# Decode attention: key, value and head-weight loads split by partitions over two DMA queues

## The chip, the cores and the metric

The kernel runs on one core of a Trainium2 chip. The metric is the time of one execution on the device, in microseconds (us); the median of three runs of the kernel before is 1301.6 us (1301.52 to 1301.69). A core has TensorE (PE in the profile), VectorE (DVE), ScalarE (ACT), GpSimd (POOL) and SyncE (SP), which run their own instruction streams, and 16 DMA engines that move data between the device memory (HBM) and the on-chip memory of 128 partitions (SBUF). SyncE and ScalarE each have a DMA queue: an instruction on the engine issues a transfer, and the 16 DMA engines carry it out.

## The reference

One step of decoding for two sequences: a layer norm, an attention over a cache of 8192 keys and values in each of 16 heads, and a gated bilinear feed-forward block behind a second layer norm.

```
B, Sq, D = 2, 1, 448;  H, Sk, Dh = 16, 8192, 256;  F = 1792;  all float32
xn = layernorm(x)
q = (xn @ wq) as [B, H, 1, Dh]
p = softmax(einsum("bhqd,bhkd->bhqk", q, k_cache) / 16)
h = x + einsum("bhqk,bhkd->bhqd", p, v_cache) as [B, 1, H * Dh] @ wo
hn = layernorm(h)
out = h + ((hn @ w_gate) * (hn @ w_up)) @ w_down
```

The two caches are 32 x 8 MiB each; with the weights 561 MB are read once and used once.

## The kernel before

The work is a loop over 32 units, one for each head and sequence (unit i is head i // 2, sequence i % 2). A unit's keys are one transfer of 8.39 MB, 64 KB in each of 128 partitions (a partition holds 64 consecutive keys of 256 numbers), and its values are another. There are two key buffers that overlap by 16 of 64 columns, so that the next keys may be written once VectorE has read the first part of the present ones, and one value buffer.

For unit n:

1. VectorE multiplies the first quarter of the keys (16 columns) by the query and sums it, then the other three quarters; the scores go to `s`. Each part is a product (`tensor_mul`, 128x4096 or 128x12288) and a sum (`tensor_reduce`). The first product waits for the keys.
2. `softmax(n - 1)`, the softmax of the unit before, lies between the first product and the first sum: a maximum on VectorE (`nm`), a small matmul, and two ScalarE instructions (`nb`, and the exponentials `p`).
3. `mix(n - 1)`: TensorE weighs the values of the unit before with `p` into `o_ps` in 32 steps; it waits for the values (event `e_v`).
4. `mixed(n - 1)`: ScalarE copies `o_ps` to `o_sb`, TensorE turns it, ScalarE scales it to `oT`. Every second unit adds its head to the output, and every fourth computes the next queries (`queries`; ScalarE writes `q`).

All loads but that of x stand on SyncE's queue, in this order: the head weights of the first two heads, the keys of unit 0 in two transfers (24 and 40 columns), then alternately the keys of unit n + 1 (which wait for VectorE's first sum of unit n) and the values of unit n (which wait for TensorE's last use of the values of unit n - 1). Four transfers of head weights (`d_w_1` to `d_w_4`, 2.75 to 3.67 MB) stand behind keys 2, 10, 18 and 26. The values of units 27 to 31 are loaded in pieces (`LATE`; `EARLY` = `LOOP` = 27 is the first of these units), and the feed-forward weights follow at the end. The class `Orders` keeps the instruction list of every engine and works out the semaphore waits; `load` adds one transfer to one engine's list, and a transfer adds 16 to its semaphore when it has landed. TensorE's part of units 0 to 26 is a hardware loop, which takes events by their count.

Of the kernel before, what the change touches and what calls it, by code (L numbers as in the profile page):

```python
# [10 lines left out]
B, D, H, SK, DH, F = 2, 448, 16, 8192, 256, 1792  # L11
EPS = 1e-5
P = 128
HALF = 64
# [46 lines left out]
    (slice(HALF, P), slice(DC - 1, DC), slice(DC, DC + 1)),  # L61
)


SCRATCH = 1024
ALIGN = (2048 - SCRATCH - 4 * 32) // 4
# [2 lines left out]
EARLY = NQ - len(LATE)  # L69
LOOP = EARLY  # L70
# [4 lines left out]
class Orders:  # L75
# [88 lines left out]
    def load(self, engine, name, out, in_, reads=(), writes=(), event=None):  # L164
# [11 lines left out]
        e = self.engines[engine]  # L176
        self._add(engine, (waits, lambda: e.dma_start(out, in_), (name, 16)))  # L177

    def take(self, event, n=1):

        at = self.taken[event] = self.taken.get(event, -1) + 1
        self._learn("PE", self.events[event][at])
        s, e = self.sem(event), self.nc.tensor
        self._add("PE", ({}, lambda: e.wait_ge(s, n), (event, -n)))  # L184
# [32 lines left out]
def decode_block(nc, x, k_cache, v_cache, w, wg, wu, wd, out):  # L217
    o = Orders(nc)
    o.sem("d_out")

    def sb(name, *shape):
        return nc.alloc_sbuf_tensor(name, list(shape), F32)[:]
# [12 lines left out]
    def act(out, in_, fn, r=(), w=(), event=None, **kw):  # L235
        put("ACT", "activation", out, in_, fn, r=r, w=w, event=event, **kw)

    def mm(out, lhsT, rhs, start, stop, r=(), w=(), mark=None, **kw):
        put("PE", "matmul", out, lhsT, rhs, start=start, stop=stop, r=r, w=w, mark=mark, **kw)
# [8 lines left out]
    w_sb = sb("w_sb", P, WALL)  # L248
    buffers = {"k": k_sb, "v": v_sb}
# [17 lines left out]
    def keys(cache, i, lo, hi):  # L267
        h, b = divmod(i, B)
        return cache[b, h].rearrange("(p j) d -> p j d", p=P)[:, lo:hi, :]

    def load_keys(name, cache, i, lo, hi, buf, at, event=None):
        o.load(
            "SP", name, buffers[buf][:, at : at + hi - lo, :], keys(cache, i, lo, hi),
            writes=[(buf, at * DH, (at + hi - lo) * DH)], event=event,
        )

    def k_base(i):
        return i % 2 * (NJ - OVER)

    def load_k(i, lo=0, hi=NJ):  # L280
        load_keys(f"d_k_{i}_{lo}", k_cache, i, lo, hi, "k", k_base(i) + lo)

    def v_parts(i):
        got, lo = [], 0
        for n, place in LATE[i - EARLY] if i >= EARLY else ((NJ, None),):
            buf, at = place or ("v", lo)
            got.append((lo, lo + n, buf, at))
            lo += n
        return got

    def load_v(i, part):
        lo, hi, buf, at = part
        load_keys(f"d_v_{i}_{lo}", v_cache, i, lo, hi, buf, at, "e_v" if i < LOOP else None)

    def load_w(name, k, lo, hi, event=None):
        o.load("SP", name, w_sb[:, lo:hi], w[k][:, lo:hi], writes=[("w", lo, hi)], event=event)

    def wq_at(hp):
        return hp % 2 * WQ
# [1 line left out]
    def wo_at(h):  # L301
        return 2 * WQ + h % 4 * WO
# [59 lines left out]
    for c in range(DC):  # L362
# [9 lines left out]
        w=["xc_x"],  # L372
# [14 lines left out]
    def q_at(h):  # L387
        return h % 2 * (1 + h // 2 % 2)

    for k in range(2):  # L390
        for b in range(B):
            for c in range(DC):
                at = c * 2 * DH + (k * DH if c < DC - 1 else 0)
# [3 lines left out]
                    w=[f"q_ps{b}"], mark="PE" if c == DC - 1 else None,  # L397
                )
            at = q_at(k)
# [19 lines left out]
    def other(i):  # L419
        return i % 2 if i >= LOOP else 0  # L420

    def event(name, i):
        return name if i < LOOP else None

    def take(name, i, n=1):
        if i < LOOP:
            o.take(name, n)
# [10 lines left out]
    def common(i):  # L438
        return piece(i, always if i == 0 else gone)

    def at_turn(i):
        return piece(i, turn_of.get(i, gone))
# [9 lines left out]
    def scores(i, part, between=None):  # L452
        h, b = divmod(i, B)
        s, name = s_t[i % 2], f"s{i % 2}"
        lo, hi = score_parts(i)[part]
        at = k_base(i) + lo
        kt = k_sb[:, at : at + hi - lo, :]
        qk, there = kt, ("k", at * DH, (at + hi - lo) * DH)
        if i == 0 and part == 0:
            qk, there = v_sb[:, : hi - lo, :], ("v", 0, (hi - lo) * DH)  # L460
        q, slot = qs[b], q_at(h)
        here = ("k", at * DH, (at + hi - lo) * DH)
        dve(
            "tensor_mul", qk, kt, q[:, slot, :][:, None, :].to_broadcast([P, hi - lo, DH]),
            r=[here, (f"q{b}", slot, slot + 1)], w=[there],
        )
        if between is not None:
            between()
        dve("tensor_reduce", s[:, lo:hi], qk, axis=AX.X, op=ALU.add, r=[there], w=[(name, lo, hi)])
# [27 lines left out]
    def mix(i, parts):  # L497
        k = other(i)
        with common(i):
            take("e_v", i, 16)  # L500
            for lo, hi, buf, at in parts:
                for t in range(lo // 2, hi // 2):
                    g, j = 32 * (t % 4), at + 2 * t - lo
                    mm(
                        o_ps[k][g : g + 2, :], p_t[k][:, 2 * t : 2 * t + 2],
                        buffers[buf][:, j : j + 2, :], t < 4, t >= NJ // 2 - 4,
                        r=[f"p{k}", (buf, j * DH, (j + 2) * DH)], w=[f"o_ps{k}"],
                        mark="PE" if t == hi // 2 - 1 else None,
                    )

    def mixed(i):
        h, b = divmod(i, B)
        k = other(i)
        act(o_sb, o_ps[k], AF.Copy, r=[f"o_ps{k}"], w=["o_sb"], event=event("e_o", i))
        with common(i):
            take("e_o", i)
            for c in range(2):
                for j in range(2):
                    mm(
                        oT_ps[:, c : c + 1], o_sb[:, (2 * j + c) * P : (2 * j + c + 1) * P],  # L520
                        sel[:, j : j + 1], j == 0, j == 1, r=["o_sb", "sel"], w=["sm1"],
                        mark="PE" if c == 1 and j == 1 else None,
                    )
        act(oT[:, :, b], oT_ps, AF.Copy, scale=rl_t[i % 2], r=["sm1", f"rl{i % 2}"],
            w=[("oT", b, b + 1)], event=event("e_oT", i))
        with common(i):
            take("e_oT", i)
        if b == B - 1 and h < H - 1:
            at = wo_at(h)
            with at_turn(i):  # L530
                if i % 8 == 1:
                    take("e_w", i, 16)
                for c in range(2):
                    mm(
                        acc_ps, oT[:, c, :], w_sb[:, at + c * D : at + (c + 1) * D], False,
                        h == H - 2 and c == 1, r=["oT", ("w", at, at + WO)], w=["acc_ps"],
                        mark="PEx" if c == 1 else None,
                    )
# [48 lines left out]
    def late_guest(name, rows, *shape):  # L587
# [6 lines left out]
    pair = sb("pair", B, B, 16)  # L594
    dve("tensor_copy", pair, ident[:B, :B][:, :, None].to_broadcast([B, B, 16]), r=["ident"],
        w=["pair"])
# [16 lines left out]
    for n in range(NQ + 1):  # L613
        hp, at = divmod(n, 2 * B)
        parts = v_parts(n - 1) if n > 0 else []
        if n > 0:
            load_v(n - 1, parts[0])
        if n < NQ:
            scores(n, 0, (lambda: softmax(n - 1)) if n > 0 else None)
        else:  # L620
            softmax(n - 1)
        if late is not None:
            mix(n - 2, late)
            mixed(n - 2)
            late = None
        if n + 1 < NQ:
            load_k(n + 1)
        for part in parts[1:]:
            load_v(n - 1, part)
        if n % 8 == 1:  # L630
            k = n // 8 + 1
            load_w(f"d_w_{k}", k, WQ if k == H // 4 else 0, WALL, event("e_w", n))
        def norm_last():
            if n > 0:
                norm(n - 1)

        if n == NQ:
            norm_last()
        else:
            for part in range(1, len(score_parts(n))):  # L640
                scores(n, part, norm_last if part == 1 else None)
        if n == NQ:
            mix(n - 1, parts[:-1])
            open_sums()
            mix(n - 1, parts[-1:])
            mixed(n - 1)
        elif n + 1 < NQ and len(parts) > 1:
            late = parts[1:]
            mix(n - 1, parts[:1])
        elif n > 0:  # L650
            mix(n - 1, parts)
            mixed(n - 1)
        if at == 2 and hp + 1 < H // 2:
            queries(n - 1, hp + 1)
        if n < NQ:
            if n == 0:
                o.ops["PE"].append(lambda: turns())
            top(n)
# [4 lines left out]
    for name, t, src in (("wg", wg_t, wg), ("wu", wu_t, wu)):  # L663
        for k, half in enumerate(PIECES[name]):
            o.load("SP", f"d_{name}_{k}", t[:, half], src[:, half],
                   writes=[("k", places[name] + half.start, places[name] + half.stop)])
    at = 0
    for n in DOWN:
        o.load("SP", f"d_wd_{at}", wd_t[:, at * D : (at + n) * D], wd[:, at * D : (at + n) * D],
               writes=[("k", at * D, (at + n) * D)])  # L670
# [4 lines left out]
        writes=["out"],  # L675
# [5 lines left out]
    def project(out, out_name, t, name, k, between=None):  # L681
# [31 lines left out]
        w=["mean"])  # L713
# [11 lines left out]
        w=["sr"])  # L725
# [28 lines left out]
    def down(lo, hi):  # L754
        for k in range(lo, hi):
# [18 lines left out]
           writes=["out"])  # L774
# [83 lines left out]
```

## Time and profile before

| | |
|---|---|
| median of 3 runs | 1301.6 us |
| the profiled execution | 1301.76 us, its span 1300.3 us |
| VectorE busy | 1130.9 us (87%) |
| TensorE matmul busy | 485.6 us (37%) |
| ScalarE busy | 62.6 us (5%) |
| moved by DMA | 561.36 MB, 432 GB/s over the span |
| granted TensorE clock, mean | 0.655 |

The span runs from the first to the last instruction; some 1.5 us lie around it. The line of DMA in the profile shows in 40 slices which share of the time the 16 DMA engines had a packet under way. A row of the timeline gives start, length, engine, line, operation, output and input, and in brackets how long the engine had been idle and what ended that. An engine's name with a q (SPq, ACTq) is its queue of instructions: there the row of a DMA is the time in which the transfer is issued, not that in which it moves.

### The profile page before, as it was taken

How to read it: one execution, taken by the hardware profiler on the slowest of the kernel's cores; microseconds unless marked ns; L12 is line 12 of the kernel's file. 1: busy time of each engine (PE TensorE's matmuls, PEld its weight loads, DVE VectorE, ACT ScalarE, POOL GpSimd, SP SyncE). 2: the span in 40 equal slices, each digit the busy share in tenths (PEclk: the TensorE clock that was granted, in tenths of full speed). 3: DMA queues.
4: the chain of work that ended last, by engine and by line, in shares of the span. 5: the costliest groups of instructions: out<-in, count | busy, mean ns of one | idle time of the engine just before them, and what ended most of it. 6: DMA issues, size and time to landing. Idle time of an engine off the chain costs nothing.

```text
span 1300.3 us, 6941 instructions
## 1 busy us (share of the span) xinstructions
PE 485.6 (37%) x2972; PEld 168.4 (13%) x2972; DVE 1130.9 (87%) x275; ACT 62.6 (5%) x184; POOL 1.4 (0%) x9
## 2 busy tenths in 40 slices
PE   3035421363331633215343063433434334243267
PEld 2011100120100201002101021010111011010013
DVE  7996988888988689888889868898888897899991
ACT  1000000000000000000000000000000000000000
POOL 0000000000000000000000000000000000000000
PEclk8566756686656766558666576665766667666578
DMA  9999999999999999999999999999999999999998
GB/s 414 423 434 448 424 448 423 446 425 444 423 444 423 439 423 448 423 448 423 444 427 444 431 427 439 431 424 446 425 446 425 426 453 425 438 433 421 435 435 369
DMA packets 11992, 561.36 MB, mean 432 GB/s; under 512 B 1354, under 2 KB 1484, under 8 KB 1740
## 3 DMA queue, kind: packets, MB, share of 16 engines
q1 hardware_dynamic: 11976, 561.20, 99.7%
q8 instruction: 7, 0.11, 0.0%
q14 instruction: 5, 0.04, 0.0%
q10 hardware_dynamic: 4, 0.00, 0.0%
HBM read 561.19 MB, written 0.01 MB: 432 GB/s over the span
## 4 chain that ended last, share of the span: by engine, by line
DMA 72%; DVE 27%; issue 0%; PE 0%; SPq 0%
DMA k_sb<-in_A_k_cache_dram 70%; DVE k_sb L230 13%; DVE s L230 13%; DMA k_sb<-in_wd_dram 2%; DVE nm L230 0%; SPq L177 0%; PE y_ps L230 0%; DVE m L230 0%; PE sm L230 0%; DVE v_sb L230 0%; DVE rl L230 0%
## 5 line engine op out<-in xcount | busy, mean ns | idle before, releaser
L230 DVE TENSOR_TENSOR k_sb<-k_sb,q 128x12288 f32<-128x12288 f32 (+2 forms) x67 | 549.6, 8203 | 128.8 <-DMA k_sb<-in_A_k_cache_dram 128.7
L230 DVE TENSOR_REDUCE s<-k_sb 128x48 f32<-128x12288 f32 (+2 forms) x67 | 549.3, 8198 | 0.2
L230 PE MATMUL o_ps<-v_sb,p 128*2 128x512 f32 x2000 | 284.8, 731 | 392.9 <-PEq L184 374.1
L230 PEld LDWEIGHTS o_ps<-v_sb,p 128*2 128x2 f32 x2000 | 53.1, 96 | 596.7 <-issue 573.2
L230 PE MATMUL sm<-nm,ones 1*128 1x1 f32 x64 | 16.7, 327 | 191.9 <-PEq L184 168.5
L230 PE MATMUL sm<-ident,m 128*1 128x128 f32 x32 | 11.0, 344 | 144.9 <-PEq L184 102.1
L230 PE MATMUL q_ps<-w_sb,xb 128*128 128x256 f32 (+1 forms) x172 | 58.9, 500 | 0.0
L230 ACT ACTIVATE o_sb<-o_ps 128x512 f32<-128x512 f32 x32 | 19.1, 597 | 683.7 <-PE o_ps L230 683.7
L230 PE MATMUL sm<-sel,o_sb 128*128 128x1 f32 x256 | 33.7, 253 | 25.7 <-PEq L184 22.1
L230 PE MATMUL acc_ps<-w_sb,oT 128*2 128x448 f32 x60 | 36.7, 750 | 15.1 <-PEq L184 9.9
L230 PEld LDWEIGHTS sm<-nm,ones 1*128 1x128 f32 x64 | 14.7, 284 | 201.5 <-issue 176.7
L230 PEld LDWEIGHTS sm<-sel,o_sb 128*128 128x128 f32 x256 | 31.8, 195 | 56.1 <-issue 46.5
L230 PEld LDWEIGHTS q_ps<-w_sb,xb 128*128 128x128 f32 x172 | 33.3, 198 | 29.9 <-issue 27.5
L230 PE MATMUL sm<-lsum,ones 128*128 128x1 f32 x64 | 17.7, 346 | 26.0 <-PEq L184 22.3
L230 ACT ACTIVATE nb<-sm 128x1 f32<-128x1 f32 x32 | 5.5, 171 | 416.0 <-PE sm L230 416.0
L230 PEld LDWEIGHTS sm<-ident,m 128*1 128x1 f32 x32 | 2.6, 80 | 157.2 <-issue 111.2
L230 PEld LDWEIGHTS sm<-lsum,ones 128*128 128x128 f32 x64 | 15.8, 307 | 27.9 <-issue 23.8
L230 ACT ACTIVATE q<-q_ps,rstd 128x512 f32<-128x512 f32 (+1 forms) x18 | 11.5, 640 | 71.4 <-PE q_ps L230 71.4
L230 PE MATMUL o_ps<-k_sb,p 128*2 128x512 f32 x48 | 9.4, 944 | 6.0 <-DMA k_sb<-in_A_v_cache_dram 6.0
L230 ACT ACTIVATE p<-s,nb 128x64 f32<-128x64 f32 x32 | 11.1, 347 | 1.0
L230 DVE TENSOR_TENSOR v_sb<-k_sb,q 128x6144 f32<-128x6144 f32 x1 | 6.6, 6557 | 4.8 <-DMA k_sb<-in_A_k_cache_dram 4.8
L230 DVE TENSOR_REDUCE total<-o_ps 128x1 f32<-128x128 f32 x1 | 0.3, 292 | 11.8 <-PE o_ps L230 11.8
(79 smaller groups left out, 95.2 us busy)
## 6 DMA issues: line engine op xcount, KB each, us to landing
v_sb<-in_A_v_cache_dram SPq DMA_DIRECT2D x4, 4096.0 KB, 30.5
w_sb<-in_w_dram SPq DMA_DIRECT2D x3, 3584.0 KB, 37.7
v_sb<-in_A_v_cache_dram SPq DMA_DIRECT2D x1, 7168.0 KB, 26.3
v_sb<-in_A_v_cache_dram SPq DMA_DIRECT2D x1, 6144.0 KB, 28.2
k_sb<-in_A_k_cache_dram SPq DMA_DIRECT2D x1, 5120.0 KB, 24.4
v_sb<-in_A_v_cache_dram SPq DMA_DIRECT2D x2, 2048.0 KB, 28.6
k_sb<-in_A_v_cache_dram SPq DMA_DIRECT2D x1, 4096.0 KB, 36.2
k_sb<-in_B_w_gate_dram SPq DMA_DIRECT2D x1, 3136.0 KB, 32.1
```

Source lines behind the costliest of these rows:

```text
L230: o.put(engine, lambda: f(*args, **kw), r, w, mark, event)
```

## The change

A new function `pair` adds a transfer to two engines' lists at once: partitions 0 to 63 on SyncE's queue, partitions 64 to 127 on ScalarE's. Each half adds 16 to the same semaphore, and whoever needs the load waits for 32. Keys of units 1 to 27, values of units 0 to 26 and the head weights `d_w_1` to `d_w_4` go this way: 27 + 27 + 4 = 58 loads. The keys of unit 0, the first head weights, and all that comes behind the values of unit 26 stay whole on SyncE's queue. The code that loads the values is moved so that on ScalarE the half stands directly behind `mix` and ahead of `mixed`.

```diff
+PAIR = ("SP", "ACT")
...
+    def pair(self, name, out, in_, writes, event=None):
+        waits = {e: self._waits(e, (), writes) for e in PAIR}
...
+        if event is not None:
+            self.events.setdefault(event, []).append(clock)
+            name = event
+        else:
+            assert name not in self.value, name
+            self.value[name] = 32
+            self.marks[who] = [(1, name, 32, clock)]
+        for k, e in enumerate(PAIR):
+            rows = slice(k * HALF, (k + 1) * HALF)
+            self._add(e, (waits[e], lambda e=e, rows=rows: self.engines[e].dma_start(out[rows], in_[rows]),
+                          (name, 16)))
...
-    def load_keys(name, cache, i, lo, hi, buf, at, event=None):
+    def load_keys(name, cache, i, lo, hi, buf, at, both, event=None):
...
+        if both:
+            o.pair(name, got, src, writes, event)
+        else:
+            o.load("SP", name, got, src, writes=writes, event=event)
...
-        load_keys(f"d_k_{i}_{lo}", k_cache, i, lo, hi, "k", k_base(i) + lo)
+        load_keys(f"d_k_{i}_{lo}", k_cache, i, lo, hi, "k", k_base(i) + lo, 0 < i <= EARLY)
...
-        load_keys(f"d_v_{i}_{lo}", v_cache, i, lo, hi, buf, at, "e_v" if i < LOOP else None)
+        load_keys(f"d_v_{i}_{lo}", v_cache, i, lo, hi, buf, at, i < LOOP, event("e_v", i))
...
-            take("e_v", i, 16)
+            take("e_v", i, 32)
...
-        if n > 0:
+        if n == 1 or n - 1 > EARLY:
             load_v(n - 1, parts[0])
...
             mix(n - 1, parts)
+            if n <= EARLY:
+                load_v(n, v_parts(n)[0])
             mixed(n - 1)
```

On ScalarE, from its first queries on, this is what stood before (a `DMA` row issues a transfer; `sm` and `o_ps` are written by TensorE):

```order
L230 ACTIVATE q<-q_ps,rstd 128x256 [waits PE] x4
L230 ACTIVATE nb<-sm 128x1 [waits PE]
L230 ACTIVATE p,lsum<-s,nb 128x64 [waits ACT]
L230 ACTIVATE o_sb<-o_ps 128x512 [waits PE]
L230 ACTIVATE oT<-sm,rl 128x2 [waits DVE,PE]
```

And this is what stands at the same place now, to the end of unit 0:

```order
L252 ACTIVATE q<-q_ps,rstd 128x256 [waits PE] x4
L198 DMA k_sb<-in_A_k_cache_dram 64x16384 [waits DVE]
L198 DMA v_sb<-in_A_v_cache_dram 64x16384 [waits DVE,PE]
L252 ACTIVATE nb<-sm 128x1 [waits PE]
L252 ACTIVATE p,lsum<-s,nb 128x64 [waits ACT]
L198 DMA k_sb<-in_A_k_cache_dram 64x16384 [waits DVE]
L198 DMA w_sb<-in_w_dram 64x7168
L198 DMA v_sb<-in_A_v_cache_dram 64x16384 [waits PE]
L252 ACTIVATE o_sb<-o_ps 128x512
L252 ACTIVATE oT<-sm,rl 128x2 [waits DVE,PE]
```

The halves of keys 1, values 0, keys 2, the head weights and values 1 have come in between. The copy to `o_sb` has no wait of its own any more, since the half of the values ahead of it waits for the same matmul.

On SyncE's queue the start of the program stood so before:

```order
L177 DMA k_sb<-in_A_k_cache_dram 128x6144
L177 DMA k_sb<-in_A_k_cache_dram 128x10240
L177 DMA k_sb<-in_A_k_cache_dram 128x16384 [waits DVE]
L177 DMA v_sb<-in_A_v_cache_dram 128x16384 [waits DVE,PE]
L177 DMA k_sb<-in_A_k_cache_dram 128x16384 [waits DVE]
L177 DMA w_sb<-in_w_dram 128x7168
L177 DMA v_sb<-in_A_v_cache_dram 128x16384 [waits PE]
```

And so it stands now:

```order
L179 DMA k_sb<-in_A_k_cache_dram 128x6144
L179 DMA k_sb<-in_A_k_cache_dram 128x10240
L198 DMA k_sb<-in_A_k_cache_dram 64x16384 [waits DVE]
L198 DMA v_sb<-in_A_v_cache_dram 64x16384 [waits DVE,PE]
L198 DMA k_sb<-in_A_k_cache_dram 64x16384 [waits DVE]
L198 DMA w_sb<-in_w_dram 64x7168
L198 DMA v_sb<-in_A_v_cache_dram 64x16384 [waits PE]
```

The order on SyncE and its waits are the same; from keys 1 on each transfer is half as large.

More of the change, by code (lines that the diff above doesn't have):

```diff
@@ L177, in load @@
         self._add(engine, (waits, lambda: e.dma_start(out, in_), (name, 16)))
+    def pair(self, name, out, in_, writes, event=None):
+        waits = {e: self._waits(e, (), writes) for e in PAIR}
+        who = ("DMA", name, len(self.marks))
+        clock = {who: 1}
+        for e in PAIR:
+            for k, n in self.known[e].items():
+                clock[k] = max(clock.get(k, 0), n)
+        self._note(who, 1, (), writes)
+        if event is not None:
[9 more added lines that the diff above has]
+                          (name, 16)))
     def take(self, event, n=1):
@@ L269, in keys @@
         return cache[b, h].rearrange("(p j) d -> p j d", p=P)[:, lo:hi, :]
-    def load_keys(name, cache, i, lo, hi, buf, at, event=None):
[L272 to L275, printed above, removed]
+    def load_keys(name, cache, i, lo, hi, buf, at, both, event=None):
+        got, src = buffers[buf][:, at : at + hi - lo, :], keys(cache, i, lo, hi)
+        writes = [(buf, at * DH, (at + hi - lo) * DH)]
+        if both:
+            o.pair(name, got, src, writes, event)
+        else:
+            o.load("SP", name, got, src, writes=writes, event=event)
     def k_base(i):
@@ L292, in load_v @@
         lo, hi, buf, at = part
-        load_keys(f"d_v_{i}_{lo}", v_cache, i, lo, hi, buf, at, "e_v" if i < LOOP else None)
+        load_keys(f"d_v_{i}_{lo}", v_cache, i, lo, hi, buf, at, i < LOOP, event("e_v", i))
     def load_w(name, k, lo, hi, event=None):
-        o.load("SP", name, w_sb[:, lo:hi], w[k][:, lo:hi], writes=[("w", lo, hi)], event=event)
+        got, src, writes = w_sb[:, lo:hi], w[k][:, lo:hi], [("w", lo, hi)]
+        if k > 0:
+            o.pair(name, got, src, writes, event)
+        else:
+            o.load("SP", name, got, src, writes=writes)
     def wq_at(hp):
@@ L531, in mixed @@
                 if i % 8 == 1:
-                    take("e_w", i, 16)
+                    take("e_w", i, 32)
                 for c in range(2):
```

## The prediction

> **What bounds the kernel now.** I read the page first: the busy shares, the line of DMA, the queues and the shares of the chain that ended last.
>
> ```profile
> span 1300.3 us, 6941 instructions
> PE 485.6 (37%) x2972; PEld 168.4 (13%) x2972; DVE 1130.9 (87%) x275; ACT 62.6 (5%) x184; POOL 1.4 (0%) x9
> DMA  9999999999999999999999999999999999999998
> DMA packets 11992, 561.36 MB, mean 432 GB/s; under 512 B 1354, under 2 KB 1484, under 8 KB 1740
> q1 hardware_dynamic: 11976, 561.20, 99.7%
> DMA 72%; DVE 27%; issue 0%; PE 0%; SPq 0%
> ```
>
> The DMA engines have a packet under way in every slice, nearly all of it from one queue (q1, SyncE's), and the chain lies on transfers for 72%. VectorE's 87% comes close, so I looked at the loop in order of time. One unit of the chain (start, length, what):
>
> ```profile
> 534.85 29.67 DMA k_sb<-in_A_k_cache_dram
> 564.51 0.02 issue
> 564.54 4.43 DVE k_sb L230
> 568.97 0.19 DVE nm L230
> 569.15 4.34 DVE s L230
> 573.51 29.62 DMA k_sb<-in_A_k_cache_dram
> ```
>
> A unit takes 573.51 - 534.85 = 38.66 us. VectorE's 9 us stand in the chain only because they release the next keys; whether they cost anything is told by the rate at which bytes move meanwhile. By stretches (length, busy time of PE, PEld, DVE, ACT and POOL, PE's clock, DMA share, GB/s), three blocks of six units each, and two stretches with a neighbour:
>
> ```profile
> 140.07:371.82 231.75, 81.73 (x494) 26.94 (x494) 210.08 (x43) 10.21 (x32) 0.00 (x0) 0.65 1.00 434
> 457.57:689.40 231.83, 81.33 (x494) 26.81 (x494) 210.08 (x43) 10.21 (x32) 0.00 (x0) 0.65 1.00 434
> 775.18:1007.00 231.82, 85.88 (x494) 27.42 (x494) 210.08 (x43) 10.20 (x32) 0.00 (x0) 0.63 1.00 434
> 371.82:410.49 38.67, 11.56 (x77) 3.72 (x77) 35.02 (x8) 1.47 (x5) 0.00 (x0) 0.63 0.98 424
> 410.49:457.57 47.08, 21.52 (x101) 7.60 (x101) 35.01 (x8) 2.85 (x7) 0.00 (x0) 0.68 1.02 443
> ```
>
> The blocks agree within 0.04% at a share of 1.00 and 434 GB/s, 27.1 GB/s for each of 16 engines. (The 424 and 443 are packets of 64 KB counted across a border; together they are 434 again.) So the loop is bound by a fixed rate of transfer, and the queue never runs dry. How much slack each issue has, the timeline of one unit tells:
>
> ```profile
> 534.85 0.33 SPq L177 DMA_DIRECT2D k_sb<-in_A_k_cache_dram  x1
> 545.34 9.45 PE L230 MATMUL o_ps<-v_sb,p 128*2 128x512 f32 x64 [12.76 <-PEq L184]
> 554.86 0.33 SPq L177 DMA_DIRECT2D v_sb<-in_A_v_cache_dram  x1
> 554.86 0.60 ACT L230 ACTIVATE o_sb<-o_ps 128x512 f32<-128x512 f32 x1 [22.98 <-PE o_ps L230]
> 564.54 4.43 DVE L230 TENSOR_TENSOR k_sb<-k_sb,q 128x4096 f32<-128x4096 f32 x1 [3.61 <-DMA k_sb<-in_A_k_cache_dram]
> 569.89 0.17 ACT L230 ACTIVATE nb<-sm 128x1 f32<-128x1 f32 x1 [12.96 <-PE sm L230]
> 570.09 0.35 ACT L230 ACTIVATE p<-s,nb 128x64 f32<-128x64 f32 x1
> ```
>
> Keys issued at 534.85 find the values before them moving until 545.3, where the matmuls on these start: 10.5 us of cover. Values issued at 554.86 find the keys moving until 564.5: 9.7 us.
>
> **The change part by part.** *Bytes.* They stay. Only their queues, and which partitions are served at one moment, change. The halves run from the end of keys 0 to the landing of values 26. The start, with the one transfer on ScalarE's queue that the trace has:
>
> ```profile
> 0.73 0.54 ACTq L177 DMA_DIRECT2D v_sb<-in_A_x_dram  x1
> 19.35 6.55 DVE L230 TENSOR_REDUCE s<-v_sb 128x24 f32<-128x6144 f32 x1
> 26.00 0.33 SPq L177 DMA_DIRECT2D v_sb<-in_A_v_cache_dram  x1
> 26.03 10.82 DVE L230 TENSOR_TENSOR k_sb<-k_sb,q 128x10240 f32<-128x10240 f32 x1
> 56.83 0.33 SPq L177 DMA_DIRECT2D k_sb<-in_A_k_cache_dram  x1
> 64.75 9.11 PE L230 MATMUL o_ps<-v_sb,p 128*2 128x512 f32 x64 [10.19 <-PEq L184]
> 1101.08 9.76 PE L230 MATMUL o_ps<-v_sb,p 128*2 128x512 f32 x64 [12.71 <-PEq L184]
> ```
>
> Keys 0 have landed at 26.03; the matmuls on values 26 start at 1101.08. That makes 1075 us of transfer in halves, and every 1% of its rate is 10.8 us.
>
> *Issues on ScalarE.* 58 more instructions at 0.33 us (SyncE's rows) to 0.54 us (its own): 19 to 31 us on an engine that is busy 62.6 us of 1300. Where they stand: the keys' half comes behind `nb` and `p`, which are over at 570.4, and waits for the sum that ends at 573.5; next behind it are the values' half and `o_sb`, 20 us later, which wait for the same matmuls. So `o_sb` is later by at most 0.54 us. Behind it hangs, in every fourth unit, the longest string: queries on TensorE, then the turn of the maximum, for which VectorE's `nm` waits:
>
> ```profile
> 604.51 0.27 PE L230 MATMUL sm<-ident,m 128*1 128x128 f32 x1
> 607.57 0.19 DVE nm L230
> ```
>
> 2.8 us lie between; 0.54 fits. Cost 0; without that cover it would be 0.54 us in each of 7 units, 4 us at most. The half itself, late by 0.54 us against SyncE's, has the 9.7 us of above.
>
> *More and smaller transfers.* 58 more, each with its own completion. The price of a transfer more is bounded by the unit with head weights: 47.08 - 38.66 = 8.42 us for 3.67 MB, where 434 GB/s asks for 8.45. So a transfer more costs no more than some 0.03 us beyond its bytes, and two queues could hide as much: 58 x 0.03 = 1.7 us either way. I take 0.
>
> *The start.* The half of keys 1 on ScalarE's queue waits for VectorE's product, over at 19.35, and then moves at once, while the second part of keys 0 has 6.65 us left on SyncE's. Shared by bytes, that part lands up to 6.65 us later; shared packet by packet, where its packets are 40 KB against 64 KB, up to 64/40 x 6.65 = 10.6 us. VectorE's string from 26.03 to the issue at 56.83 moves with it, to 63.5 or 67.5. The DMA engines have values 0 until 64.75, so the 7.9 us of cover become 1.2, or are gone and 2.7 us of transfer are lost. Besides, ScalarE's queue then runs dry first, and for some 5.5 us a half moves alone; at half the rate that loses another 2.7 us. Bounds 0 and 5.4; I take 1.5, nearer to nothing, since no row shows a lone half to be slower.
>
> *The end.* From keys 28 on all is whole on SyncE's queue as before. Cost 0.
>
> *The rate while halves move.* No row shows a transfer of 64 partitions; all large ones have 128. From below: the fixed 434 GB/s, whatever the other engines do, excludes a gain beyond the seams unless the limit is in the queue itself. From above: two halves that get in each other's way altogether move one behind the other at half of the rate. The nearest rows, all of them, stand at 434; I take 434 and keep the other end for the range.
>
> [...]
>
> Sum, against the profiled execution: 1301.8 + 0 + 0 + 1.5 + 0 = 1303.3 us. The median of the runs lies 0.2 lower, so 1303.1.
>
> **The rivals.** *Full collision.* Before, each of 16 engines carries its own 8 of the 128 partitions of a transfer. A half leaves 4 to each, so two engines must share what one had to itself, if the limit of 27.1 GB/s belongs to where the bytes go and not to the engine. Each engine takes packets from the two queues in turn. Both halves are issued by the same event, so all engines begin with the same half, and after a packet of 64 KB all change to the other: half of the ways idle at any moment. Then 1075 us become 2150, and the time is 1303 + 1075 = 2378. For it: the fixed rate looks like a clocked path; the queues never run dry, so nothing breaks the step. Against it: rows cannot tell an engine's limit from a destination's. It decides the sign from 0.25% of the rate on (2.6 of 1075 us), as no cover stands behind the DMA engines themselves. [...]
>
> *Partial collision.* The same, but the two engines that share are out of step. If one trails by a fraction d of a packet, a packet takes 2 - d times as long as alone; over all d the mean is 1.5, so 538 us more: 1841. Engines that get ahead would widen d and end at 1.1 (1410), and every load waits for its slowest pair, which pulls towards 2.
>
> *Faster.* If part of the limit is the single queue (a gap between packets that a second queue fills), 0.5% of rate gives 1075 x 0.005 = 5.4 us: 1297.7. Against it: the head weights' 8.42 us show no gap, and a share of 1.00 leaves none to see. [...]
>
> **How the numbers follow.** This measurement can tell about 0.2%, 2.6 us, from no change. No collision: 0.44, with 1300 to 1307 as its own range, of which 0.28 within 0.2% and 0.16 above, since the start's 0 to 5.4 us lie across the bound. Faster: 0.13. Partial collision: 0.23. Full collision: 0.20. So faster 0.13, same 0.28, slower 0.16 + 0.23 + 0.20 = 0.59. The likeliest single case is no collision, 1303.1, though cases above it hold more together. The range has to take in full collision, as without it more than 2 in 10 is left out at 0.20 and the tail below: 1296 (0.5% of rate, and seams hidden) to 2380.
>
> **What the profile after would show.** If right: units of 38.6 to 38.7 us at 434 GB/s; two queues that carry about 328 and 233 MB, the latter half of the 58 loads (54 of 8.39 MB and four of 13.8 MB together); VectorE's wait for keys still near 3.6 us; ScalarE's waits for `o_ps` shorter by nothing that the chain shows; the second part of keys 0 landing between 26 and 37 us. With a collision: the DMA line still full of nines, since a packet that is held up counts as under way, but 200 to 400 GB/s in slices 2 to 33 and units of 42 to 77 us, VectorE waiting for keys by the difference; and from keys 28 on 38.6 us and 434 GB/s again. If the units stay and the total grows, the start is at fault: a gap in DMA share between 58 and 70 us. What would make the forecast wrong is above all the rate with 64 partitions, for which the trace of before has no row.

## The result and the profile after

The changed kernel takes 2416.8 us (median of four runs, 2415.8 to 2428.8) against 1301.6 us: 1.859 times the time, with an interval of 1.853 to 1.865. The forecast was 1303.1, in a range of 1296 to 2380.

The page of the changed kernel, in the lines that answer to those of before:

```profile
span 2414.5 us, 7000 instructions
DMA  9999999999999999999999999999999999999999
GB/s 292 208 217 208 209 220 214 208 208 221 214 208 218 211 221 210 208 219 215 208 212 219 212 210 216 216 218 208 209 219 215 208 218 215 215 214 285 435 426 389
DMA packets 12920, 561.36 MB, mean 232 GB/s; under 512 B 2282, under 2 KB 2412, under 8 KB 2668
q1 hardware_dynamic: 8264, 327.82, 54.6%
q10 hardware_dynamic: 4644, 233.38, 45.3%
another core or an unknown queue 50%; DVE 43%; DMA 7%; issue 0%; PE 0%; SPq 0%; DVEq 0%
```

The bytes are the same and the DMA line has its nines as before, but the line of GB/s has halved while halves move, and is back at 435 in the slice after the last of them. The busy share says that packets are under way, not how fast they go. q1 and q10 (ScalarE's queue) carry 328 and 233 MB, as forecast. The chain puts half of the span down to "another core or an unknown queue": it does not name what released VectorE there, so the rows of one unit are read instead.

One unit in the loop, from issue of keys to issue of keys, and then its stretch and the next by rate (columns as in the prediction):

```profile
909.15 0.47 SPq L198 DMA_DIRECT2D k_sb<-in_A_k_cache_dram  x1
909.15 0.50 ACTq L198 DMA_DIRECT2D k_sb<-in_A_k_cache_dram  x1
939.62 9.45 PE L252 MATMUL o_ps<-v_sb,p 128*2 128x512 f32 x64 [32.74 <-PEq L206]
949.14 0.47 SPq L198 DMA_DIRECT2D v_sb<-in_A_v_cache_dram  x1
978.82 4.42 DVE L252 TENSOR_TENSOR k_sb<-k_sb,q 128x4096 f32<-128x4096 f32 x1 [43.59 <-DMA k_sb<-in_A_k_cache_dram]
987.79 0.47 SPq L198 DMA_DIRECT2D k_sb<-in_A_k_cache_dram  x1
```

```profile
909.15:987.79 78.64, 11.95 (x77) 3.81 (x77) 35.01 (x8) 1.47 (x5) 0.00 (x0) 0.54 1.00 213
987.79:1066.44 78.65, 15.01 (x81) 4.20 (x81) 35.01 (x8) 1.47 (x5) 0.00 (x0) 0.54 1.00 213
2243.71:2279.91 36.20, 11.28 (x69) 2.63 (x69) 35.02 (x8) 1.13 (x4) 0.00 (x0) 0.59 0.98 425
```

A unit takes 78.65 us instead of 38.66, at 213 GB/s instead of 434. The issues are where they were: both halves of the keys leave at 909.15, right behind VectorE's sum. VectorE's wait for keys has grown from 3.6 to 43.6 us. The last row, behind the halves, is back at 425 GB/s.

Where the time went, the trace's records of single packets tell. A packet here is the part of one partition, 64 KB in a whole load as in a half. Packets that start where another ended were taken as one DMA engine's; one such string before, and one after (durations in us; `a` is ScalarE's queue, a point the completion of a transfer):

```
before  2.42 2.42 2.42 2.42 2.42 2.42 2.42 2.42 .
after   4.87 . 5.11 a4.86 . a5.12 4.88 a4.86 4.85 a4.85 4.87 . 5.12 a4.86 . a5.12
```

Of the 6207 packets of 64 KB that start between 140 and 1100 us, all but 11 took 2.42 us before (at most 2.95). After, the 6834 in halves that start from 45 us on take 4.92 on average (nine in ten between 140 and 1100 us at least 4.85). An engine carries 54 x 8 = 432 of them: 432 x (4.92 - 2.42) = 1080 us. An engine's 24 packets of 28 KB from the head weights rose from 1.06 to 2.05 us and its 8 of 21 KB from 0.80 to 1.50: 29 us more. That is 1109 of the 1114 us between the two profiled executions (2415.95 and 1301.76).

### The profile page after: what moved, and what is told of

Read it like the earlier page. It is cut to its first block, busy times and chain, and to the rows that moved or that the text cites. A ratio compares the mean times of both kernels' runs of the same rounds, so it can differ in the third digit from the quotient of the medians.

```text
span 2414.5 us, 7000 instructions
## 1 busy us (share of the span) xinstructions
PE 498.5 (21%) x2972; PEld 173.7 (7%) x2972; DVE 1131.0 (47%) x275; ACT 62.6 (3%) x184; POOL 1.4 (0%) x9
## 4 chain that ended last, share of the span: by engine, by line
another core or an unknown queue 50%; DVE 43%; DMA 7%; issue 0%; PE 0%; SPq 0%; DVEq 0%
DVE k_sb L252 21%; DVE s L252 21%; DMA k_sb<-in_A_k_cache_dram 5%; DMA k_sb<-in_wd_dram 1%; DVE m L252 0%; DVE nm L252 0%; DVE rl L252 0%; SPq L179 0%; PE y_ps L252 0%; PE sm L252 0%; DVE v_sb L252 0%; DVEq L232 0%
## 5 line engine op out<-in xcount | busy, mean ns | idle before, releaser
L252 PE MATMUL q_ps<-w_sb,xb 128*128 128x256 f32 (+1 forms) x172 | 64.6, 536 | 0.0
L252 PE MATMUL sm<-sel,o_sb 128*128 128x1 f32 x256 | 34.6, 256 | 39.8 <-PEq L206 36.2
L252 PE MATMUL q_ps<-k_sb,xr 128*32 128x256 f32 (+3 forms) x96 | 9.8, 498 | 1.9 <-DVE v_sb L252 1.9
L252 ACT ACTIVATE oT<-sm,rl 128x2 f32<-128x2 f32 x32 | 8.4, 262 | 39.9 <-PE sm L252 39.9
## 6 DMA issues: line engine op xcount, KB each, us to landing
v_sb<-in_A_v_cache_dram SPq DMA_DIRECT2D x1, 7168.0 KB, 26.1
```

Of the source, the lines that this page charges most:

```text
L252: o.put(engine, lambda: f(*args, **kw), r, w, mark, event)
```

## The experiments

**Cut by columns.** In `pair`, the rows stay whole and the columns are cut (`n` is half of the columns; three dots stand for what is left out of a line, here and below):

```diff
-            rows = slice(k * HALF, (k + 1) * HALF)
-            ... dma_start(out[rows], in_[rows])
+            cols = slice(k * n, (k + 1) * n)
+            ... dma_start(out[:, cols], in_[:, cols])
```

> The same 58 loads, the same two queues and the same places in the order, but cut by columns: each half has all 128 partitions and half of each partition's bytes. Theory 'ways' (the bytes of a packet enter by a way that belongs to its partition, the ways of partitions 0 to 63 are half of all, and the engines work through the two halves one behind the other): the halves reach all ways, units of 38.7 us at 434 GB/s, 1301 to 1306 us. Rival 'queues' (taking turns between two queues halves the rate): as with the change, units of 78.7 us, some 2417 us. Rival 'few partitions' (a transfer of 64 partitions is slow as such, whatever partitions they are): 1301 to 1306 us as well.

Measured: 1304.2 us, ratio 1.0020 (1.0011 to 1.0029). Two queues and as many transfers of the same size, with twice as many packets of half the size, at full rate (the page, then a row of the timeline):

```profile
GB/s 405 428 434 435 434 435 434 432 431 433 431 434 435 435 434 435 434 434 432 432 435 430 433 435 435 434 434 435 435 432 432 426 437 447 427 436 429 435 432 370
q10 hardware_dynamic: 8356, 233.38, 41.5%
```

```profile
28.63 10.83 DVE L253 TENSOR_TENSOR k_sb<-k_sb,q 128x10240 f32<-128x10240 f32 x1 [2.76 <-DMA k_sb<-in_A_k_cache_dram]
```

Its packets of 32 KB took 1.21 us on both queues, half of 2.42. "Queues" has fallen. What is left is 2.6 us. The second part of keys 0 lands 2.6 us later (28.63 against 26.03), but this is not where the time goes. By the trace's packets, this kernel has moved its first 25 MB, at 60 us, only 0.1 us later than the kernel before; from there the delay grows evenly, by some 0.3 us with every 50 MB, to 2.8 us at 480 MB, where the cut loads end, and then stays as it is. So the loss goes with the smaller packets of the cut loads: one of 32 KB takes 1.213 us where half of a 64 KB one is 1.209. Over 1075 us these 0.3% are enough for it; no run varies the size of the packets by itself.

**The halves on one queue.** Both halves go to SyncE, one behind the other:

```diff
-        for k, e in enumerate(PAIR):
+        for k in range(2):
...
+            self._add("SP", ...
```

> The halves by partitions stay, but both stand on SyncE's queue, one behind the other. 'Ways': the rate is that of one half at a time, half of 434 GB/s; 1301.6 + 1075 = 2377 us, and up to 2417 if the 0.33 us by which each half is longer than that with the change (78.65 / 4 = 19.66 against 19.33) come from the halves and not from the second queue. 'Queues': one queue again, 1302 us. 'Few partitions': 2377 to 2417 us.

Measured: 2478 us, ratio 1.904 (1.901 to 1.908), above what was expected.

```profile
500.00:1000.00 500.00, 90.11 (x512) 30.45 (x512) 206.76 (x42) 11.50 (x34) 0.00 (x0) 0.58 1.00 208
```

(A stretch of the loop, columns as before.) The second queue is not needed for the loss, and softens it a little: 208 GB/s against 213. The packets say why: 5.07 us on average against 4.92. The excess over twice 2.42 does not come from the second queue; it grows without it.

**Three cuts: 32, 64 and 32 partitions.** On SyncE's queue:

```diff
+        for lo, hi in ((0, 32), (32, 96), (96, 128)):
+            ... dma_start(out[lo:hi], in_[lo:hi])
```

> Each of the 58 loads in three transfers on SyncE's queue: partitions 0 to 31, 32 to 95, 96 to 127. The middle one has 64 partitions, as many as a half, but 32 of them below 64 and 32 above. [...] 'Few partitions': all three at half of the rate or less, 2377 us and above. 'Queues': 1302 us.

Measured: 2357 us (1.811, 1.808 to 1.814), near what "few partitions" asked for. But the packets do not say that. The string of one engine, in the order outer, middle, outer:

```
4.88 5.12 . 3.79 2.83 2.42 2.43 . 4.76 5.03 .
```

In this string the middle packets fall to 2.42 us, as if the neighbours had left by then; the outer ones take 4.8 to 5.1. And the engines have gone out of step, with gaps in the DMA share (0.90):

```profile
500.00:1000.00 500.00, 93.25 (x516) 31.44 (x515) 210.07 (x42) 11.61 (x34) 0.00 (x0) 0.58 0.90 221
```

So this run decides nothing by its time, since transfers that move at different rates (packets of 2.42 and of 4.8 to 5.1 us) overlap in it. Cleaner ones follow.

**Even and odd partitions.** The change itself, with another choice of 64 partitions:

```diff
-            ... dma_start(out[rows], in_[rows])
+            ... dma_start(out[k::2], in_[k::2])
```

> Two queues and halves of 64 partitions as with the change, but SyncE's half has the even partitions and ScalarE's the odd ones, so each half reaches partitions on both sides of 64. 'Ways' in its simple form (all that counts is which ways a transfer reaches): 1302 to 1306 us. [...] 'Queues' and 'few partitions': 2417 us.

Measured: 1303.4 us, ratio 1.0013 (1.0002 to 1.0023). Two queues, 64 partitions in each half, the same packets of 64 KB, and of the loss 1.8 us are left (the page, a row of the timeline, two stretches):

```profile
q10 hardware_dynamic: 4644, 233.38, 41.4%
```

```profile
31.26 10.83 DVE L251 TENSOR_TENSOR k_sb<-k_sb,q 128x10240 f32<-128x10240 f32 x1 [5.12 <-DMA k_sb<-in_A_k_cache_dram]
```

```profile
64.70:140.07 75.37, 31.86 (x178) 11.37 (x178) 65.59 (x14) 4.32 (x12) 0.00 (x0) 0.68 0.98 425
141.78:691.28 549.50, 201.17 (x1166) 66.08 (x1166) 490.15 (x99) 24.74 (x76) 0.00 (x0) 0.65 1.00 434
```

The second part of keys 0 lands at 31.26, and the stretch behind it moves 425 GB/s at a DMA share of 0.98: the start that the prediction feared. By the packets, 1.3 of the 1.8 us are lost here, between 60 and 72 us, and 0.3 more over the whole loop. From 140 us on nearly all packets took 2.42 us, on both queues. Fourteen units take 549.50 us at 434 GB/s; the same stretch before, from 140.07 to 689.40, is 549.33. "Few partitions" has fallen.

**One half of the values, with nothing beside it.** Two kernels made from that of before: everything on SyncE's queue, and the values of units 1 to 26 in one transfer of 64 partitions. The values of the other 64 are left out, so these two kernels do less than the others and serve to be compared with each other. The second has 32:96 in both places:

```diff
+        if 0 < i < LOOP:
+            o.load("SP", ..., v_sb[0:64], keys(v_cache, i, 0, NJ)[0:64], ...)
```

> The kernel before, everything on SyncE's queue and uncut, except that of the values of units 1 to 26 only partitions 0 to 63 are loaded, in one transfer (the other half of these values is left out). There is no second half and no second queue that it could collide with. 'Ways, inside one transfer' (its 16 engines meet two by two on 8 ways): a packet of 64 KB takes 4.8 to 5.1 us instead of 2.42, 4 packets an engine take as long as 8 did, and half of the values' bytes saves nothing: units of 38.7 us, 1302 to 1310 us. Rival 'between halves' (only two halves that move at once or in turn hinder each other): 4 packets of 2.42 us, 29 us of transfer in a unit, VectorE with 35.0 us becomes the bound, 1185 to 1215 us.

> The same, with partitions 32 to 95 instead of 0 to 63: as many partitions, bytes, packets and transfers. 'Ways' (partitions below 64 use one half of the ways, those above the other): the transfer reaches all ways, a packet takes 2.42 us, a unit has 29 us of transfer and is bound by VectorE's 35.0 us: 1185 to 1215 us. Rival 'halves as such' (64 partitions one behind the other are slow wherever they lie): 1302 to 1310 us, as with partitions 0 to 63.

Measured: 1426 us with partitions 0 to 63 (1.096, 1.088 to 1.103), 1174.0 us with 32 to 95 (0.902, 0.900 to 0.904). As many bytes, packets, partitions and transfers, on one queue; 252 us lie between. The first moves 109 MB less than the kernel before and is slower than it. Landing times of the values (median, us) of the first and the second:

```profile
v_sb<-in_A_v_cache_dram SPq DMA_DIRECT2D x27, 34.0
```

```profile
v_sb<-in_A_v_cache_dram SPq DMA_DIRECT2D x27, 24.5
```

Stretches of both, and VectorE's wait for keys in the first:

```profile
268.00:600.00 332.00, 108.03 (x599) 36.20 (x599) 252.51 (x52) 13.66 (x42) 0.00 (x0) 0.62 0.94 287
```

```profile
200.30:340.12 139.82, 60.10 (x340) 19.66 (x336) 139.68 (x29) 7.26 (x22) 0.00 (x0) 0.67 0.85 360
```

```profile
DVE k_sb L230 <- DMA k_sb<-in_A_k_cache_dram: 264.2, 25, 35.2
```

With 32 to 95, VectorE is busy for 139.68 of 139.82 us: it has become the bound, and the DMA engines have time to spare. The packets of the values take 2.42 us there, and 5.1 with 0 to 63 (the first of an engine's four less, 4.2 to 5.0). The slowness belongs to one transfer and to which partitions it covers. It needs neither a second half nor a second queue. One thing no run separates: row p of the source always goes to partition p, so a limit at the source's addresses would hit the same transfers. Against it speaks that the head weights slowed by nearly the same factor in the change (1.06 to 2.05 us), though their halves are 1.8 MB from another tensor and those of keys and values 4.2 MB.

1174 is 11 us below the range expected, and 1426 is above its 1302 to 1310. The units of the first are 44 us, where 4 x 5.1 + 8 x 2.42 = 39.8 us an engine would do. Some 2 us of the difference are pauses, in which the queue has run dry: of the 43 us that the engines stand idle between 193 and 1126 us, 42 lie within 8 us before an issue of keys and 3 us behind it. One unit shows how:

```profile
380.38 0.33 SPq L177 DMA_DIRECT2D k_sb<-in_A_k_cache_dram  x1
397.56 0.47 SPq L177 DMA_DIRECT2D v_sb<-in_A_v_cache_dram  x1
422.25 0.33 SPq L177 DMA_DIRECT2D k_sb<-in_A_k_cache_dram  x1
```

The last packet of the keys issued at 380.38 ended at 402.2, and 14 of the 16 engines' completions were in by then. The other two came at 406.45 and 412.34, behind packets of the values, so VectorE began only at 413.28 and the next keys left at 422.25, when nearly all of the values had been moved. Before, the 16 completions of such a load come within 1.6 us, and with 32 to 95 within 0.8. Why two of them come so late is open; the other 2 us of a unit are packets of whole loads that take 2.5 us and more where they meet a half. That mixing costs more than its sum was seen again:

**Keys alone in halves.** The change with `both` false for the values and the head weights.

> The change for the keys alone: keys 1 to 27 in halves by partitions over two queues, values and head weights whole on SyncE's queue. 'Ways': only the 27 x 8 packets of the keys on each engine take 4.93 instead of 2.42 us: 1301.6 + 27 x 8 x 2.51 = 1844 us, and somewhat more if a late engine's half meets the next whole load. If two queues with halves of either kind were needed to slow the loads: well below 1844.

Measured: 1994 us in the faster of two runs, 150 us above the sum of 1844 (the other took 2041). The direction holds, the sum does not: as with partitions 0 to 63 of the values, whole loads and halves together cost more than their packets alone. Where these 150 us lie was not settled.

**Even and odd, with a start that waits.** ScalarE's half of keys 1 waits for the second part of keys 0:

```diff
+        if name == "d_k_1_0":
+            waits["ACT"]["d_k_0_0"] = 16
```

> Halves by even and odd partitions over two queues as before (1303.4 us), and ScalarE's half of keys 1 waits for the second part of keys 0 to land, so that it no longer takes turns with it. If what is left of that kernel's 1.8 us is the start: the second part of keys 0 lands at 26.0 instead of 31.3 us and the time is that of the kernel before, 1301.6 +- 0.7 us. If it is the second queue in the loop: 1303.4 us.

Measured: 1301.97 us against 1301.58, ratio 1.0003 (0.9994 to 1.0012).

```profile
26.14 10.82 DVE L253 TENSOR_TENSOR k_sb<-k_sb,q 128x10240 f32<-128x10240 f32 x1
```

The part lands at 26.1 again, and 1.4 of the 1.8 us are gone; the 0.4 that are left lie within the interval of no change. This is the idea of the change without its two costs, and it gains nothing: none of the versions beats the kernel before.

## Why the prediction was wrong

*The step that failed* is "The rate while halves move". It took 434 GB/s from rows that all have 128 partitions, and kept the half rate for the range. Measured, 213 GB/s: a packet of 64 KB in a half takes 4.92 us instead of 2.42, and with the head weights this makes 1109 of the 1114 us lost. The prediction had said that no row of before shows a transfer of 64 partitions; it then let the nearest rows decide, though they were far in the one respect that the change alters.

*The likeliest case* was given 0.44, full collision 0.20. The mechanism of full collision was right in its core: the limit of 27.1 GB/s does not belong to the engine alone but goes with the partitions (halves on one side of partition 64 moved at 213 GB/s, whole loads at 434). Partitions 32 to 95 and the even partitions, at 2.42 us a packet, show it; so do partitions 0 to 63, at 5.1 with no other half near. That the sharing takes place where the bytes go and not where they come from is argued above, not shown.

*Its size* was 2378, and 2417 was measured, outside the range. The mis-sized term is the price of a shared packet: 4.92 us, not twice 2.42. With 2 x 2.42 the halves would take 432 x 0.08 = 35 us less and the time would be 2382.

*Its reason* holds as far as the trace shows. Full collision had two engines of the same half share, while the ways of the other half lie idle because all engines change halves together. The engines do take turns between the queues packet by packet, and they are in step: counted every 0.1 us from 140 to 2190 us, 14.6 of the 16 engines are on the same half on average. On one queue, where the halves come one behind the other anyway, the loss is the same and more. Whether engines out of step would lose less, as partial collision had it, no run shows.

*Right:* the issues on ScalarE cost nothing (both halves leave at 909.15, the same moment; `o_sb` comes 0.54 us later, as said; the kernel with the wait has these issues too and takes 1301.97 us); more transfers cost next to nothing in the loop (549.50 against 549.33 us) as long as the packets keep their size; the second queue brings nothing (1301.97 against 1301.58 us with the wait); the end is as before (a unit behind the halves takes 36.20 us at 425 GB/s, where the same one took 36.26 at 423). *The start*, 1.5 us in bounds of 0 to 5.4, cost 1.3 us with even and odd halves, and the wait removed it; with halves by columns, where the cover of 7.9 us was enough for a landing 2.6 us late, it cost 0.1. The no-collision sum of 1303.1 us comes within 0.3 us of what the even and odd halves measured, 1303.4: the sum was right for another choice of partitions.

## What to carry to other kernels

Where a kernel is bound by transfers, ask of each transfer which partitions it writes, before how many there are or which queue they stand on: here a packet of 64 KB to partitions 0 to 63 took 5.1 us, one to 32 to 95 or to every second partition 2.42, as in a load of all 128. When a change alters a property that no row of the profile varies, the nearest row is not evidence for it; give the far end the weight that its mechanism earns, or ask for a run. And read the GB/s beside the busy share: nines in the DMA line stood over 434 GB/s and over 213.

## What the runs showed of the hardware that was not expected

- A packet of 64 KB takes 2.42 us in a load of all partitions, of 32 to 95 or of every second one. In halves on one side of partition 64 it takes 4.92 us with two queues taking turns and 5.07 us on one queue; what makes the 2 to 5% above twice 2.42 was not tried.
- The issue of a half of 64 partitions took 0.47 us on SyncE's queue where a whole load took 0.33.
- Whole loads and halves on one side of partition 64, mixed in one stream, cost more than their sum: 1426 where 1302 to 1310 was expected, 1994 where 1844. The DMA share fell to 0.94 and, with three cuts, to 0.90. In the run of 1426 us the engines waited for the next issue of keys; in the unit looked at, it was late because two of 16 completions came 4 and 10 us behind the data. Why these come late is open.
- Cut by columns, the same bytes in twice as many packets of half the size cost 2.6 us, spread over the 1075 us in which they move.
